# A retention layer and two feed-forward layers on one core: the decays of v and of the state as GpSimd multiplications

## The chip, the core and the metric

The kernel runs on one core of one Trainium2 chip. A core has a matrix engine (TensorE; PE in the profile, PEld for its weight loads), three engines for elementwise work (VectorE or DVE, ScalarE or ACT, GpSimd or POOL), a queue engine that issues most transfers (SyncE, SP), and 16 DMA engines that all queues share. The metric is device time in microseconds of one execution, as the median of several; lower is better.

## The reference

```python
scores = q @ k.T / sqrt(64)                      # q, k, v: 8 batches, 8 heads, 576 positions, 64 wide
gamma = 1 - 2.0 ** (-5 - head)                   # one decay per head
ret = scores * where(i >= j, gamma ** (i - j), 0)
x = (ret @ v) as 4608 tokens x 512
h = x @ w_in;  x = (h - tanh(h)) @ w_out         # first feed-forward layer, 512 -> 2048 -> 512
h = x @ w_in2; out = (h * sigmoid(1.702 * h)) @ w_out2   # second one
```

The decay is separable: `gamma ** (i - j)` is a factor of the key's position times a factor of the query's position. The kernel puts the key's factor on v.

## The kernel before, in words

**Chunks of the retention.** Each batch's 576 positions are cut into five chunks of 128, 128, 128, 128 and 64, so there are 40 chunks, and the first four of them (all of batch 0) are done ahead of the feed-forward work. For a chunk the kernel loads kT, qT, v and k (`att_load`), multiplies v by its decay (`att_decay`), multiplies kT by qT into `pj` and masks it into `pm` on VectorE (`att_scores`), and then (`att_values`) adds two products into `op`: `pm` with the decayed v, and, from the second chunk of a batch on, the state `S` with qT. A third product, `up`, of k with the decayed v is added to the old state (L352), and the sum is multiplied by gamma to the 128th (L353): this is the state for the next chunk. `op` times `dq` is the chunk's output, `xf` for the tokens of the first tile and `xe` later. A chunk whose decayed v is late holds up its `up` and its `op`; a late state holds up the `op` of the next chunk.

**Who multiplies v.** For the first eight chunks it is one VectorE instruction (L295; 512 elements a partition, 256 for a batch's last chunk). From the ninth on it is ScalarE, one instruction for each head or pair of heads (L300: eight of 64 elements, four for a last chunk). The state is decayed on VectorE always.

**Layer 1.** A tile is 512 tokens. Its x is cut into a 16-bit high half `xh` (ScalarE, L186) and low half `xl` (VectorE, L187), the weights likewise into `wih`, `wil`, `woh`, `wol`, and each product is taken as three matmuls (high-high, low-high, high-low): L464 for `h`, L626 for `y`. The weights come as 64-bit numbers, in 16 pieces of 1 MB (eight of w_in, eight of w_out, called units): `unit_join` puts one together into a 32-bit `w` (ScalarE L176 and, for w_out, L180; VectorE L178, L181, L182), `unit_split1` cuts it into halves (L186, L187). A unit's load waits for a buffer that an earlier join has to free. All this runs in the first tile, beside chunks 4 to about 8. `act1` makes the activation: two tanh and a square on ScalarE (L477, L478, L481), a product (L482) and the halves `gh` and `gl`. The `h` banks are two: the third block of 12 `h` matmuls waits until ScalarE has read both tanh of the first block, and so on.

**Layer 2** begins at about 800 us (L520, L555) and takes no part in the change.

**What sets the order.** The program is written as a list of steps, but a scheduler that plans with its own timings orders the instructions of each engine, and each engine then works strictly in that order. To hold the scheduler back, the code writes one element of a tile that a later instruction fills, from a value that must be there first: such a pin makes the later instruction wait. Two loads have pins on GpSimd (L158: one element of `xf` copied into `f`). Where TensorE would be idle in the first 31 us, matmuls on a tile of zeros (`idle`, L704 and L719) keep it busy.

Of the kernel before, what the change touches and what calls it, by code (L numbers as in the profile page):

```python
# [17 lines left out]
AF = mybir.ActivationFunctionType  # L18
ALU = mybir.AluOpType
# [5 lines left out]
B, H, S, D = 8, 8, 576, 64  # L25
NT, DM, DFF = 4608, 512, 2048
P = 128
# [4 lines left out]
NPAIR = H // 2  # L32
CHUNKS = [(s0, min(P, S - s0)) for s0 in range(0, S, P)]
# [22 lines left out]
LEAD = 4  # L56
# [39 lines left out]
def small_h(ctx: ExitStack, tc: tile.TileContext, w1i, w1o, w2i, w2o, qt, kt, k, v, dq_d,  # L96
            dv_d, mask_d, dg_d, out, flag):
    nc = tc.nc
    V, A, G, PE, SP = nc.vector, nc.scalar, nc.gpsimd, nc.tensor, nc.sync
# [85 lines left out]
    def two(hi, lo, src, scale):  # L185
        A.activation(out=hi, in_=src, func=AF.Copy, scale=scale)  # L186
        V.scalar_tensor_tensor(out=lo, in0=src, scalar=scale, in1=hi, op0=ALU.mult, op1=ALU.subtract)  # L187

    def unit_split1(kind, p):
        o, w = L[1], L[1].raw.pop((kind, p))  # L190
        if kind == "i":
            b, u = divmod(p, 2)
            if not u:
                o.wih[b], o.wil[b] = (wp1.tile([P, KD, 512], F16, tag=f"{nm}{b}", name=f"{nm}1_{b}") for nm in ("wih", "wil"))
            hi, lo = (x[b][:, :, u * 256 : u * 256 + 256] for x in (o.wih, o.wil))
        else:
            b, u = divmod(p, 4)
            if not u:
                o.woh[b], o.wol[b] = (wp1.tile([P, 8, DM], F16, tag=f"{nm}{b}", name=f"{nm}1_{b}") for nm in ("woh", "wol"))
            hi, lo = (x[b][:, 2 * u : 2 * u + 2, :] for x in (o.woh, o.wol))  # L200
        two(hi, lo, w, SW)

    def unit_most1(kind, p):
# [62 lines left out]
    def ps_tile(pp, stage, name):  # L266
        p, tag = pp[stage]
        return p.tile([P, NPAIR, P], F32, tag=tag, name=name)

    def ps_two(pp, stage, name):  # L270
        p, tag = pp[stage]
        return p.tile([P, 2, NPAIR, P], F32, tag=tag, name=name)
# [17 lines left out]
    def att_decay(b, n):  # L290
        s0, T = CHUNKS[n]
        a = att[b, n]
        if b * len(CHUNKS) + n < 2 * LEAD:
            x, w = (0, H) if T == P else (H, NPAIR)
            V.tensor_tensor(out=a.v[:, :w], in0=a.v[:, :w], op=ALU.mult,  # L295
                            in1=dg[:, x : x + w].rearrange("p (a b) -> p a b", b=1).to_broadcast([P, w, D]))
            return
        for h in range(H if T == P else NPAIR):
            x = h if T == P else H + h
            A.activation(out=a.v[:, h], in_=a.v[:, h], func=AF.Copy, scale=dg[:, x : x + 1])  # L300

    def att_scores(b, n, pp, pin=None):
        s0, T = CHUNKS[n]
# [20 lines left out]
    def att_values(b, n, pp):  # L324
        s0, T = CHUNKS[n]
        a = att.pop((b, n))
        op = ps_two(pp, "v", "op")
        state = att.get((b, "S"))

        def add(w, x, c0, c1, start, stop):  # L330
            for hp in range(NPAIR):
                q, c = divmod(hp, 2)
                for j in range(2):
                    PE.matmul(op[64 * c : 64 * c + 64, j, q, c0:c1], w(hp, j), x(hp, j), start=start and not q, stop=stop and q == 1)  # L334

        half = lambda j: slice(64 * j, 64 * j + 64)
        if n:
            add(lambda hp, j: state[half(j), hp, :], lambda hp, j: a.qT[half(j), hp, :T], 0, T, True, False)
        if T == P:
            add(lambda hp, j: a.v[half(j), NPAIR * j + hp, :], lambda hp, j: a.p[j][half(j), hp, :64], 0, 64, not n, False)  # L340
            add(lambda hp, j: a.v[:, NPAIR * j + hp, :], lambda hp, j: a.p[j][:, hp, 64:], 64, P, False, True)
        else:
            add(lambda hp, j: a.v[half(j), hp, :], lambda hp, j: a.p[0][half(j), hp, :T], 0, T, not n, True)
        if n + 1 < len(CHUNKS):
            up = ps_tile(pp, "u", "up") if pp is not late else op[:, 0, 2:].rearrange("p a (b d) -> p (a b) d", b=2)
            for hp in range(NPAIR):
                for j in range(2):
                    PE.matmul(up[half(j), hp, :D], a.k[:, NPAIR * j + hp, :], a.v[:, NPAIR * j + hp, :], start=True, stop=True)  # L348
        if n + 1 < len(CHUNKS):
            new = ap.tile([P, NPAIR, D], F32, tag="S", name="S")  # L350
            if n:
                V.tensor_tensor(out=new, in0=up[:, :, :D], in1=state, op=ALU.add)  # L352
            V.tensor_tensor(out=new, in0=new if n else up[:, :, :D], op=ALU.mult,  # L353
                            in1=dg[:, H + NPAIR :].rearrange("p (a b) -> p a b", b=1).to_broadcast([P, NPAIR, D]))
            att[b, "S"] = new
        by_bank = lambda x, at: x.rearrange("p (j q) t -> p j q t", j=2)[:, :, :, at : at + T]
        done, g0 = 0, b * S + s0
        if g0 + T <= TT:

            if not x_first:  # L360
                x_first.append(yp.tile([P, KD, TT], F32, tag="yf", name="xf"))
            V.tensor_tensor(out=by_bank(x_first[0], g0), in0=op[:, :, :2, :T], in1=by_bank(dq, 0), op=ALU.mult)
            return
        e = ap.tile([P, NPAIR, P], F32, tag="xe", name="xe", bufs=1)
        if n + 1 < len(CHUNKS):
            V.tensor_copy(out=e[:, 0, :1], in_=new[:, 0, :1])
        V.tensor_tensor(out=by_bank(e, 0), in0=op[:, :, :2, :T], in1=by_bank(dq, 0), op=ALU.mult)
        while done < T:
            ti, off = divmod(g0 + done, TT)
            m = min(T - done, TT - off)  # L370
            SP.dma_start(x_d[ti][:, :, off : off + m], e[:, :, done : done + m])
            done += m
# [293 lines left out]
    dg = ac.tile([P, H + 2 * NPAIR], F32, name="dg")  # L666
# [11 lines left out]
    early = {"s": (ps_y, "y"), "v": (ps_a, "a"), "u": (ps_h, "h")}  # L678
# [3 lines left out]
    units1 = deque([("i", 0), ("i", 1), ("o", 0)])  # L682
# [8 lines left out]
    def next_join(after=None):  # L691
        unit_join(1, *units1[0], wb, after)
        next_load()

    def next_split():
        unit_split1(*units1.popleft())

    warm = cp.tile([P, TT], F16, name="warm")
    V.memset(warm, 0.0)
# [21 lines left out]
    for i in range(-2, LEAD):  # L721
        if i + 2 < LEAD:
            att_decay(*chunks[i + 2])
        if 0 <= i + 1 < LEAD:
            att_scores(*chunks[i + 1], early)
        if i >= 0:
            att_values(*chunks[i], early)
            if i == 0:
                att_load(*beyond[NIP])
                for x in range(2):  # L730
                    next_load(tp, x_first[0][:1, x, :1])
            if i in (1, LEAD - 1):
                fill(att[0, "S"][:1, 0, :1], 5 if i == 1 else 12)
        if i == 2:
            after = [att[0, LEAD - 1].p[-1][:1, 0, :1]]
# [2 lines left out]
        pre.popleft()()  # L738
    for i in range(2):
        next_join(after[i])  # L740
        next_split()
    for i in range(1, LEAD):
        att_load(*beyond[i + NIP])
    bg = deque()
    for i, ch in enumerate(chunks[LEAD:]):
        def begin(ch=ch, nxt=beyond[LEAD + i + NIP - 1] if i else None):
            if nxt:
                att_load(*nxt)
            att_decay(*ch)

        bg.append(begin)
        pp = middle if i < 2 else late
        pin = (lambda: att[0, "S"][:1, 0, :1], lambda: newest[0][:1])[i] if i < 2 else None
        bg.append(lambda ch=ch, pp=pp, pin=pin: att_scores(*ch, pp, pin))
        bg.append(lambda ch=ch, pp=pp: att_values(*ch, pp))
# [6 lines left out]
    for i in range(n1 + LAG):  # L762
        if i < n1:
            t, p = steps[i]
# [3 lines left out]
            for _ in range(2 if len(pre) > KF // 2 - p else 1):  # L768
                if pre:
                    pre.popleft()()  # L770
            work = [f for _ in range(2 if units1 else 0) for f in (next_join, next_split)]
            if bg:
                n = min(6 if t == 0 else 5, len(bg))
# [46 lines left out]
        if i >= LAG:  # L820
            t, p = steps[i - LAG]
# [4 lines left out]
    for n in range(LAG, NTILE * KF // 2):  # L826
        t, p = divmod(n, KF // 2)
# [827 lines left out]
```

## Time and profile before

| | |
|---|---|
| median of 3 runs | 1558.76 us (1558.08 to 1559.37) |
| the profiled execution | 1558.13 us, of which its span is 1556.4 us |
| PE busy | 1531.8 us (98%) |
| DVE, ACT busy | 1082.1 us (70%), 823.1 us (53%) |
| POOL busy | 4.9 us in 18 instructions |

Rows of a timeline begin with the start and the duration in us, then the engine, the line of the kernel, the operation and the tiles (out<-in), and in brackets how long the engine had been idle before and what ended that. Durations of instructions that follow each other overlap a little, so the distance from start to start is what one costs.

### The profile page before, as it was taken

Reading aid. Unit: us, or ns where it says so; the run is one execution under the profiler, and the core shown is the slowest. Engines: PE = TensorE matmul, PEld = TensorE weight load, DVE = VectorE, ACT = ScalarE, POOL = GpSimd, SP = SyncE. Lnnn points to the kernel's source line nnn. Section 1 sums busy time; section 2 is a strip of 40 time slices with the busy share of each in tenths; the row PEclk is TensorE's granted clock in tenths of the full one; section 3 lists DMA queues with packets and bytes.
Section 4 is the critical chain, followed back from the end, with each engine's and each line's share of the span. In section 5 each row is a group of like instructions: output and inputs, shape, how many; then the busy total and the mean of one; then the engine's idle time right before and its main releaser. Section 6 shows DMA issues by size and latency. Waiting matters only on the chain.

```text
span 1556.4 us, 29515 instructions
## 1 busy us (share of the span) xinstructions
PE 1531.8 (98%) x12347; PEld 1024.0 (66%) x12347; DVE 1082.1 (70%) x1720; ACT 823.1 (53%) x1441; POOL 4.9 (0%) x18
## 2 busy tenths in 40 slices
PE   7999999999999999999999999999999999999998
PEld 4444555555554544444444588888888888888887
DVE  6984535554443438888776499797888888887865
ACT  3995545455455446778676455354544454454432
POOL 0000000000000000000000000000000000000000
PEclk9999999999999999999999999999999999999999
DMA  9663324233323124444428243433434433432310
GB/s 356 219 197 123 118 74 155 73 105 109 112 79 106 51 92 138 170 162 156 158 101 310 85 150 116 152 123 123 150 119 127 141 127 119 140 129 99 133 62 30
DMA packets 107983, 205.84 MB, mean 132 GB/s; under 512 B 24640, under 2 KB 47808, under 8 KB 105664
## 3 DMA queue, kind: packets, MB, share of 16 engines
q1 hardware_dynamic: 107552, 203.72, 39.4%
q8 instruction: 99, 1.62, 0.4%
q14 instruction: 44, 0.36, 0.1%
q10 hardware_dynamic: 288, 0.14, 0.0%
HBM read 161.88 MB, written 41.94 MB: 131 GB/s over the span
## 4 chain that ended last, share of the span: by engine, by line
PE 91%; ACT 3%; DVE 1%; DMA 1%; issue 0%; ACTq 0%; SPq 0%; DVEq 0%
PE y L626 22%; PE h L464 22%; PE pr L520 21%; PE yp L555 20%; PE op L334 2%; PE pj L316 2%; PE yk L555 1%; PE op L348 1%; DMA f<-in_moe_w_out 1%; ACT w L176 1%; ACT v L300 0%; ACT u L481 0%; ACT u L477 0%; ACT wih L186 0%; ACT w L180 0%
## 5 line engine op out<-in xcount | busy, mean ns | idle before, releaser
L520 PEld LDWEIGHTS <-ws 128*128 128x128 f16 x3024 | 295.9, 98 | 36.5 <-issue 1.7
L464 PE MATMUL h<-xh,wih 128*128 128x512 f16 x576 | 218.2, 379 | 2.2 <-ACT wih L186 1.9
L464 PE MATMUL h<-xl,wih 128*128 128x512 f16 x576 | 218.2, 379 | 0.8 <-DVE xl L187 0.8
L626 PE MATMUL y<-gl,woh 128*128 128x512 f16 x576 | 218.5, 379 | 0.0
L626 PE MATMUL y<-gh,wol 128*128 128x512 f16 x576 | 218.4, 379 | 0.0
L464 PE MATMUL h<-xh,wil 128*128 128x512 f16 x576 | 217.9, 379 | 0.4 <-DVE wil L187 0.4
L626 PE MATMUL y<-gh,woh 128*128 128x512 f16 x576 | 218.2, 379 | 0.0
L520 PE MATMUL pr<-th,ws 128*128 128x256 f16 x1152 | 217.4, 273 | 0.3 <-DVE u L534 0.2
L626 PEld LDWEIGHTS <-woh 128*128 128x128 f16 x1152 | 112.2, 98 | 133.0
L464 PEld LDWEIGHTS <-wih 128*128 128x128 f16 x1152 | 111.0, 98 | 133.3 <-ACT wih L186 2.0
L482 DVE TENSOR_TENSOR wt<-u,wt 128x1024 f32<-128x1024 f32 x72 | 88.1, 1224 | 150.6 <-ACT u L481 150.6
L555 PE MATMUL yp<-wo,gh 128*128 128x256 f16 x1152 | 186.8, 273 | 0.0
L520 PE MATMUL pr<-bh,ws 128*128 128x256 f16 x864 | 170.4, 273 | 0.0
L477 ACT ACTIVATE u<-h 128x512 f32<-128x512 f32 x144 | 84.9, 590 | 158.2 <-PE h L464 158.1
L536 ACT ACTIVATE gs<-u,isig 128x1024 f32<-128x1024 f32 x72 | 82.5, 1146 | 142.6 <-DVE u L535 142.6
L520 PE MATMUL pr<-tl,ws 128*128 128x256 f16 x576 | 157.0, 273 | 0.0
L555 PE MATMUL yp<-wo,gl 128*128 128x256 f16 x576 | 135.4, 273 | 0.0
L186 ACT ACTIVATE gh<-gs,sg 128x1024 f16<-128x1024 f32 x72 | 82.7, 1149 | 91.5 <-DVE gs L539 91.3
L555 PE MATMUL yp<-wo,ringwoh 128*128 128x256 f16 x768 | 126.2, 273 | 0.0
L555 PEld LDWEIGHTS <-gh 128*128 128x128 f16 x1152 | 112.7, 98 | 13.0
L520 PE MATMUL pr<-bl,ws 128*128 128x256 f16 x432 | 117.4, 273 | 0.0
L186 ACT ACTIVATE gh<-wt 128x1024 f16<-128x1024 f32 x72 | 76.0, 1055 | 73.7 <-DVE wt L482 73.5
(141 smaller groups left out, 2317.7 us busy)
## 6 DMA issues: line engine op xcount, KB each, us to landing
ws<-pd SPq DMA_DIRECT2D x144, 448.0 KB, 3.9
f<-in_moe_w_in SPq DMA_DIRECT2D x16, 1024.0 KB, 5.8
f<-in_moe_w_out SPq DMA_DIRECT2D x16, 1024.0 KB, 5.1
yd<-ev SPq DMA_DIRECT2D x36, 256.0 KB, 2.6
yf<-yd SPq DMA_DIRECT2D x9, 1024.0 KB, 5.7
out<-ev SPq DMA_DIRECT2D x36, 256.0 KB, 2.6
kT<-t_k SPq DMA_DIRECT2D x32, 256.0 KB, 2.9
qT<-t_q SPq DMA_DIRECT2D x32, 256.0 KB, 2.8
```

The costliest lines, as they stand in the source:

```text
L176: A.activation(out=half[:, :, 1].bitcast(F16), in_=part[:, :, 3].bitcast(BF16), func=AF.Copy)
L186: A.activation(out=hi, in_=src, func=AF.Copy, scale=scale)
L316: PE.matmul(o, a.kT[hs, hp, :T], a.qT[hs, hp, :T], start=True, stop=True)
L334: PE.matmul(op[64 * c : 64 * c + 64, j, q, c0:c1], w(hp, j), x(hp, j), start=start and not q, stop=stop and q == 1)
L348: PE.matmul(up[half(j), hp, :D], a.k[:, NPAIR * j + hp, :], a.v[:, NPAIR * j + hp, :], start=True, stop=True)
L464: PE.matmul(h, w, x[:, kd, :], start=n == 0, stop=n == 3 * KD - 1)
L477: A.activation(out=u[:, x], in_=h, func=AF.Tanh, scale=isig * NARROW)
L482: V.tensor_tensor(out=w, in0=u, in1=th, op=ALU.mult)
L520: PE.matmul(ps, w, x[:, xi, k, :], start=i == 0, stop=i == 5)
L536: A.activation(out=gs.rearrange("p (a b) n -> p a b n", b=2)[:, 0:4:3], in_=h.rearrange("p (a b) n -> p a b n", b=2), func=AF.Gelu_apprx_s ...
L555: PE.matmul(bank[:, m], ops[a][:, x, m * P : m * P + P], L[2].out[w][:, p, wi, :], start=start and m == 0 and r == 0, stop=stop and m == 1 ...
L626: PE.matmul(ys[m], a, b, start=first and i == 0, stop=last and i == 2)
```

## The change

v's decay is one multiplication for every chunk, on GpSimd for all but the very first chunk of all (`b or n`), which stays on VectorE. ScalarE no longer has a part in it. The state's decay goes to GpSimd for the second to fourth chunk of batch 0 (`n and pp is early`). The first unit's low halves get a pin: one element of `wil` is written from `after[1]`, the last element of `xf`, so that VectorE makes `wil` only behind chunk 3's output. Nothing else changes in the program as written, but the scheduler orders the first tile anew.

```diff
-    def unit_split1(kind, p):
+    def unit_split1(kind, p, after=None):
...
+        if after is not None:
+            V.tensor_copy(out=lo[:1, 0, :1], in_=after)
         two(hi, lo, w, SW)
...
     def att_decay(b, n):
         s0, T = CHUNKS[n]
         a = att[b, n]
-        if b * len(CHUNKS) + n < 2 * LEAD:
-            x, w = (0, H) if T == P else (H, NPAIR)
-            V.tensor_tensor(out=a.v[:, :w], in0=a.v[:, :w], op=ALU.mult,
-                            in1=dg[:, x : x + w].rearrange("p (a b) -> p a b", b=1).to_broadcast([P, w, D]))
-            return
-        for h in range(H if T == P else NPAIR):
-            x = h if T == P else H + h
-            A.activation(out=a.v[:, h], in_=a.v[:, h], func=AF.Copy, scale=dg[:, x : x + 1])
+        x, w = (0, H) if T == P else (H, NPAIR)
+        (G if b or n else V).tensor_tensor(out=a.v[:, :w], in0=a.v[:, :w], op=ALU.mult,
+                                           in1=dg[:, x : x + w].rearrange("p (a b) -> p a b", b=1).to_broadcast([P, w, D]))
...
-            V.tensor_tensor(out=new, in0=new if n else up[:, :, :D], op=ALU.mult,
-                            in1=dg[:, H + NPAIR :].rearrange("p (a b) -> p a b", b=1).to_broadcast([P, NPAIR, D]))
+            by = G if n and pp is early else V
+            by.tensor_tensor(out=new, in0=new if n else up[:, :, :D], op=ALU.mult,
+                             in1=dg[:, H + NPAIR :].rearrange("p (a b) -> p a b", b=1).to_broadcast([P, NPAIR, D]))
...
-        next_split()
+        next_split(None if i else after[1])
```

GpSimd's order at the start of the program, before (`mask` is the mask of the short chunks, the two L158 are the pins of two weight loads, `ISA` at L137 loads the code of the all-reduce that follows):

```order
L709 COPY mask_133<-mask 64x64 x2
L158 COPY f_289<-xf 1x1
L158 COPY f_292<-xf 1x1
L137 ISA
L137 ISA arx<-m_7677 128x1
```

and now (`v_1` to `v_4` are the v of chunks 1 to 4, `v_0_492` that of chunk 5; the ISA at L296 loads the code that the multiplications need, and that of the all-reduce is loaded behind the last of them):

```order
L707 COPY mask_133<-mask 64x64 x2
L296 ISA
L296 TENSOR_TENSOR v_1_198<-v_1_198,dg 128x512
L296 TENSOR_TENSOR v_2_206<-v_2_206,dg 128x512
L158 COPY f_289<-xf 1x1
L158 COPY f_292<-xf 1x1
L351 TENSOR_TENSOR S<-S,dg 128x256
L296 TENSOR_TENSOR v_3_214<-v_3_214,dg 128x512
L296 TENSOR_TENSOR v_4_287<-v_4_287,dg 128x256
L351 TENSOR_TENSOR S<-S,dg 128x256 x2
L296 TENSOR_TENSOR v_0_492<-v_0_492,dg 128x512
```

The pins of the two loads now stand behind two multiplications, and the decay of chunk 2's state (the first of the two S rows) stands behind v of chunk 4, as it did on VectorE.

VectorE's order from chunk 2's output to chunk 3's, before:

```order
L362 TENSOR_TENSOR xf<-op,dq 128x4x128
L352 TENSOR_TENSOR S<-up,S 128x256
L171 COPY w_465<-pm 1x1
L295 TENSOR_TENSOR v_4_287<-v_4_287,dg 128x256
L353 TENSOR_TENSOR S<-S,dg 128x256
L178 TENSOR_SCALAR w_465<-f_218 128x1024
L352 TENSOR_TENSOR S<-up,S 128x256
L181 TENSOR_SCALAR f_218<-f_218 128x1024
L353 TENSOR_TENSOR S<-S,dg 128x256
L182 SCALAR_TENSOR_TENSOR w_465<-f_218,w_465 128x1024
L311 COPY pj_564<-S 1x1
L362 TENSOR_TENSOR xf<-op,dq 128x4x128
```

and now, two rows further (`w_465` is the first unit, `w_478` the second):

```order
L360 TENSOR_TENSOR xf<-op,dq 128x4x128
L349 TENSOR_TENSOR S<-up,S 128x256
L171 COPY w_465<-pm 1x1
L178 TENSOR_SCALAR w_465<-f_218 128x1024
L349 TENSOR_TENSOR S<-up,S 128x256
L181 TENSOR_SCALAR f_218<-f_218 128x1024
L182 SCALAR_TENSOR_TENSOR w_465<-f_218,w_465 128x1024
L308 COPY pj_565<-S 1x1
L360 TENSOR_TENSOR xf<-op,dq 128x4x128
L202 CAST wil_0_474<-xf 1x1
L171 COPY w_478<-xf 1x1
L187 SCALAR_TENSOR_TENSOR wil_0_474<-w_465,wih_0_473 128x4x256
```

Three multiplications have left this stretch, and the second L349 waits for GpSimd now, with all that stands behind it.

ScalarE's order behind the halves of x, before (`w_552` is the first unit of w_out, `w_477` the second of w_in, `w_576` the third):

```order
L176 ACTIVATE w_552<-f_289 128x1024
L180 ACTIVATE w_552<-f_289 128x1024
L176 ACTIVATE w_477<-f_220 128x1024
L186 ACTIVATE woh_0_560<-w_552 128x1024
L477 ACTIVATE u<-h 128x512
L478 ACTIVATE wt<-h 128x512
L481 ACTIVATE u,energy<-u 128x512
L186 ACTIVATE wih_0_473<-w_477 128x4x256
L477 ACTIVATE u<-h 128x512
L478 ACTIVATE wt<-h 128x512
```

and now (the same units are `w_553`, `w_478` and `w_577`):

```order
L176 ACTIVATE w_478<-f_220 128x1024
L176 ACTIVATE w_553<-f_289 128x1024
L180 ACTIVATE w_553<-f_289 128x1024
L186 ACTIVATE wih_0_473<-w_478 128x4x256
L186 ACTIVATE woh_0_561<-w_553 128x1024
L475 ACTIVATE u<-h 128x512
L476 ACTIVATE wt<-h 128x512
L176 ACTIVATE w_577<-f_292 128x1024
L479 ACTIVATE u,energy<-u 128x512
L475 ACTIVATE u<-h 128x512
L476 ACTIVATE wt<-h 128x512
```

The second unit's high halves come ahead of the first block's activation, which both used to precede them, and a join's L176 has come between the first block's tanh and the second's.

## Rows read from the trace of the kernel before

**Rows 1.** Busy us by stage: PE, PEld, DVE, ACT, POOL, clock, DMA, GB/s

```profile
20.00:31.00 11.00, 6.87 (x92) 4.57 (x89) 8.22 (x16) 4.94 (x6) 0.00 (x0) 0.84 1.07 376
39.00:60.00 21.00, 20.18 (x135) 10.28 (x136) 20.38 (x29) 21.00 (x39) 0.00 (x0) 1.00 0.57 172
100.00:118.50 18.50, 14.80 (x79) 6.89 (x78) 15.15 (x20) 16.28 (x29) 0.00 (x0) 1.00 0.45 149
```

**Rows 2.** Waits of PE after 31 us: total us, times, longest

```profile
PE op L334 <- DVE pm L321: 3.0, 2, 2.2
PE pj L316 <- issue: 1.5, 1, 1.5
```

**Rows 3.** The chain of work, 0 to 120 us: start, us, what

```profile
41.75 1.25 ACT w L176
43.01 1.20 ACT w L180
47.14 0.49 ACT wt L478
48.47 2.03 ACT v L300 x8
...
59.32 0.63 DVE f L181
...
61.67 1.15 DVE w L182
...
81.74 2.00 ACT v L300 x8
...
96.54 5.25 DMA f<-in_moe_w_out
...
106.31 1.91 ACT v L300 x8
```

**Rows 4.** Timeline of POOL, the first 13 us

```profile
4.66 0.51 POOL L709 COPY mask<-mask 64x64 f32<-64x64 f32 x2 [4.23 <-DMA mask<-c_mask]
12.23 0.29 POOL L158 COPY f<-xf 1x1 int32<-1x1 int32 x2 [7.07 <-DVE xf L362]
```

**Rows 5.** Instructions of L137: durations in ns, first and last start

```profile
L137 POOLq MODIFY_POOL_CONFIG  x2: 1/1/1, 12.5 to 12.6; - x2
```

**Rows 6.** Transfers issued in the first 14 us: KB, us to landing

```profile
v<-n_v SPq DMA_DIRECT2D x4, 256.0 KB, 5.6
...
kT<-t_k SPq DMA_DIRECT2D x1, 128.0 KB, 10.3
```

**Rows 7.** Timeline of all engines, 9 to 32 us

```profile
9.69 0.69 DVE L295 TENSOR_TENSOR v<-v,dg 128x512 f32<-128x512 f32 x1 [1.99 <-DMA v<-n_v]
...
18.25 0.67 PE L334 MATMUL op<-qT,S 64*64 64x128 f32 x16 [1.10 <-DVE xf L362]
...
23.73 0.43 DVE L295 TENSOR_TENSOR v<-v,dg 128x256 f32<-128x256 f32 x1 [2.25 <-DMA v<-n_v]
...
24.07 0.42 DVE L353 TENSOR_TENSOR S<-S,dg 128x256 f32<-128x256 f32 x1
...
24.63 1.13 PE L334 MATMUL op<-qT,S 64*64 64x128 f32 x16 [4.13 <-DVE S L353]
...
25.51 1.78 PE L334 MATMUL op<-pm,v 64*64 64x64 f32 x32
...
27.23 3.07 PE L719 MATMUL idle<-warm 128*128 128x512 f16 x12
...
27.50 0.67 DVE L362 TENSOR_TENSOR xf<-op,dq 128x512 f32<-128x512 f32 x1
...
28.57 1.99 ACT L186 ACTIVATE xh<-xf 128x1024 f16<-128x1024 f32 x2
...
29.90 1.20 DVE L187 SCALAR_TENSOR_TENSOR xl<-xf,xh 128x1024 f16<-128x1024 f32 x1
```

**Rows 8.** Timeline of PE: the third block of h

```profile
39.03 0.39 PE L464 MATMUL h<-xh,wih 128*128 128x512 f16 x1 [1.86 <-ACT wih L186]
```

More of the change, by code (lines that the diff above doesn't have):

```diff
@@ L693, in next_join, with next_split @@
         next_load()
-    def next_split():
-        unit_split1(*units1.popleft())
+    def next_split(after=None):
+        unit_split1(*units1.popleft(), after)
     warm = cp.tile([P, TT], F16, name="warm")
```

## The prediction

> **What bounds the kernel now.** I read the page first: PE is busy for 98% of the span, so no more than the 25 us in which it idles can be won, and the change touches only the first 560 us. Then I read where the idle time lies. In the first 31 us PE follows the loads; from 31 us on it waits only for VectorE and ScalarE, and only in the first tile: 1.86 us before the third block of h, which waits for ScalarE [rows 8], and, between 90 and 118.5 us, 3.0 us in two waits for VectorE's mask and 1.5 us before one pj [rows 2]. Behind 119 us no wait of layer 1 is left, so whatever ScalarE or VectorE gains there is worth nothing. Third I read the two engines by stage: from 39 to 60 us ScalarE is busy for 21.0 of 21.0 us and VectorE for 20.38; from 100 to 118.5 us PE has only 14.80 of 18.5, ScalarE 16.28 and VectorE 15.15 [rows 1]. They bound the first tile together, joining and cutting weights. Last the chain of waits: ScalarE's v decays lie on it three times, 2.03, 2.00 and 1.91 us [rows 3].
>
> **The change, part by part.** The sum is made against the profiled execution, 1558.13 us; the median is 0.63 above it.
>
> *The price of a GpSimd multiplication.* No such row exists. GpSimd's copies of 64 elements take 0.51 us for two, its copies of one element 0.29 for two [rows 4]: 0.255 and 0.145 each, so 1.7 ns an element, and 1.0 us for 512 and 0.6 for 256, the values that I take. Below stands VectorE's own 0.69 us [rows 7], above ScalarE's 2.03 us for the same work [rows 3].
>
> *The code load.* GpSimd now loads code between its mask copies, which end at 5.17 us [rows 4], and v of chunk 1, which lands at 9.69 [rows 7]. Before, the load's records of 1 ns stand at 12.5 us [rows 5] and nothing followed for 800 us, so its cost is not seen. It lies between nothing and 10.3 us, the longest transfer of that stretch; the nearest row is the median transfer, 5.6 us [rows 6], and I take that: ready at 10.8 us, v of chunk 1 done at 11.8 instead of 10.4. This lateness of 1.4 us is hidden: chunk 2's op waits 1.10 us for xf in any case, and chunk 3's op waits 4.13 us at 24.63 [rows 7], so only what exceeds some 5 us comes through. The two pins come at about 14 us instead of 12.2 [rows 4]; on SP their loads stand behind that of chunk 4's v, so they lose nothing. The Trainium skill ("GPSIMD Engine Reference", section 2.1) gives about 6 us for the first call after a load, which no run here shows yet; by it v of chunk 1 would be done at 12.2 us and the sum would stay.
>
> *The wait at 24.63 us.* It is VectorE's order: the state of chunk 2 stands behind v of chunk 4, which lands at 23.73, and op starts 0.90 later [rows 7]. The change doesn't take this away, since on GpSimd the state stands behind the same v. v 0.6, state 0.6, and the 0.14 that lay between the state's end and op (24.07 + 0.42 to 24.63): op starts 1.34 after the landing, 0.44 later than now, with bounds of 0 (VectorE's prices) and +1.2. Chunk 3's xf was 0.2 behind the end of its op (25.51 + 1.78 to 27.50) and gives that back, so xf is 0.3 late, and ScalarE, which still has the first high halves to make, starts xh at most 0.1 late. But VectorE makes xl now behind two pins, `wil` and the next join's L178, where xl came straight behind `wil` at 29.90 [rows 7], and TensorE's filling matmuls are shifted with op. I put the stream of h at +0.5.
>
> *The third block of h.* ScalarE is free at 30.56 + 0.1 (28.57 + 1.99) [rows 7]. The new order gives it L176 twice and L180, 1.25 + 1.25 + 1.20 [rows 3], until 34.35. VectorE's L181 (0.63) must follow that L180, then a mask of chunk 4 and L182 twice, 1.15 each [rows 3]: 37.6. ScalarE's `woh` (1.0, as one of the two xh) ends at 38.6 and the two tanh, 0.49 each, at 39.6. Only then is the bank of the third block free, which began at 39.03 [rows 8]. So the earlier `wih` wins nothing: the wait for it becomes a wait for the bank, and PE is 0.6 late there. A join's L176 now stands between the tanh of the first and of the second block, so I carry +0.7 to 60 us, start included, with bounds of -1.9 (the wait simply goes) and +2.5.
>
> *From 60 to 118.5 us.* ScalarE loses 2.00 + 1.91 us on the chain, and the 2.03 at 48.47 before it [rows 3]. The three PE waits, 4.5 us [rows 2], are for VectorE instructions that themselves wait for ScalarE's joins, so they shrink by what ScalarE gains. They can't all go: a weight load of 5.25 us, issued when a buffer comes free, stands on the chain too [rows 3], and ScalarE was idle there. I take two thirds, -3.0, between 0 and -4.5.
>
> *Behind that* 28 chunks go from ScalarE to GpSimd beside a PE that does not wait: 0. GpSimd's second code load, for the all-reduce, comes at about 560 us with 270 us to spare: 0. The state's decays of chunks 1 and 3 and VectorE's saved multiplications in the first 31 us: 0, since those instructions wait for loads.
>
> Sum: 1558.13 + 0.7 - 3.0 = 1555.8; with the median's 0.63, 1556.4 us.
>
> **The rivals.**
>
> *The order is better than I walked it.* If VectorE's join comes out early enough, the 1.86 us go too, with nothing lost at the start, and all 4.5 us behind: -6.1 with +0.3 for the state, 1552.7 us. For it speaks that VectorE loses seven v decays in its first 43 us and that the scheduler moved `wih` forward; against it that the bank needs ScalarE, which has no gap.
>
> *GpSimd's work holds up VectorE.* No row shows the two at work together for longer than a copy of one element. If each multiplication keeps VectorE waiting for its 1.0 us, then chunks 5 to 8 put 4.0 us on a VectorE that has 0.6 us of idle time between 39 and 60 us [rows 1], and chunks 9 to 11 take back two thirds of what ScalarE gives: +3.4 + 0.7 - 1.0, or 1561.9 us, slower. It decides from about 0.6 us per multiplication; below that VectorE's idle 3.35 us from 100 to 118.5 [rows 1] takes it. The Trainium skill ("SBUF — State Buffer", section "Who interferes with whom" and the reading of its diagram) has such a rule: the two share a port pair under an exclusive lock, which a VectorE instruction with two SBUF inputs wants too, and the loser waits for the whole instruction. By that rule xl, `wil`, L182 and the product L482 would be held, masks from PSUM not; no run here shows it.
>
> *The code load is long.* The transfers of that stretch already fill the DMA engines. From a load of some 9.5 us on, v of chunk 1 eats up the two waits, and every further us is late at the first h: at 13 us +3.5. TensorE's granted clock is a part of this: it was 0.84 on average from 20 to 31 us [rows 1], which is 3.5 us at the lower level, 1.2 GHz, behind the 4.13 us wait, and a longer wait means more of the fillers at that level. 1561.5 us.
>
> *The waits are where the loads put them*, and ScalarE's gain turns into waiting for weights: about 1558.8 us. I count this to the forecast's case, as its slow edge.
>
> **Chances.** The forecast with its slow edge 0.40, the better order 0.30, VectorE held 0.17, the long load 0.13. A measurement of this kernel tells some 0.2% from no change, 3.1 us. Faster by more than that: the better order and a little of the forecast, 0.33. Slower by more: about half of the two slow rivals and a remainder, 0.18. Within: 0.49. The range that should hold 8 in 10 is 1551.5 to 1562.5 us; the forecast's own is 1554 to 1559.5.
>
> **What would show it.** Right: GpSimd's 512-element rows at 0.7 to 1.3 us; v of chunk 1 done by 15 us; chunk 3's op at 25.0 to 25.4; the third block of h at 39.3 to 40 behind a tanh, not behind `wih`; less than 2 us of PE waits between 60 and 118.5 us. Wrong: VectorE's L182 or L187 longer than 1.2 us, or idle gaps before them, while GpSimd multiplies; a wait of PE on GpSimd before 18 us that reaches the first h; a granted clock below 1.00 behind 31 us; the third block of h at 37.5 us.

## The result: 1569.99 us, slower by 0.7%

The changed kernel takes 1569.99 us (median of 4, 1568.68 to 1570.94), the kernel before, on the same chip, 1559.07 (1558.08 to 1559.84): a ratio of 1.0069, 95% interval 1.0053 to 1.0085, or +10.8 us. The forecast was 1556.4 us, its range ended at 1562.5.

| profiled execution | before | changed |
|---|---|---|
| span, us | 1556.4 | 1567.2 |
| first h that needs `xl`, us | 31.62 | 37.79 |
| third block of h, us | 39.03 | 45.39 |
| first h of tile 1 that waits for `xl`, us | 133.91 | 144.20 |
| busy us of ScalarE, VectorE, GpSimd | 823, 1082, 5 | 771, 1084, 49 |

ScalarE lost 52 us of work and VectorE gained none worth telling; nevertheless 6.2 us are lost ahead of the first h, 4.1 more until tile 1, and 0.5 behind it. Tile 1's row, before and changed:

```profile
133.91 0.38 PE L464 MATMUL h<-xl,wih 128*128 128x512 f16 x1 [0.81 <-DVE xl L187]
```

```profile
144.20 0.38 PE L462 MATMUL h<-xl,wih 128*128 128x512 f16 x1 [0.65 <-DVE xl L187]
```

First the stages of the changed kernel, with the columns of [rows 1] (the mean granted clock stands behind the engines):

```profile
10.00:20.00 10.00, 2.85 (x42) 2.59 (x42) 1.95 (x4) 0.00 (x0) 2.90 (x6) 0.78 1.05 383
20.00:31.00 11.00, 8.75 (x190) 7.10 (x188) 5.95 (x11) 1.57 (x2) 3.17 (x5) 0.89 1.07 374
39.00:60.00 21.00, 18.09 (x127) 9.11 (x125) 20.00 (x25) 18.18 (x28) 2.09 (x2) 1.00 0.46 155
80.00:100.00 20.00, 17.61 (x139) 8.59 (x137) 16.16 (x19) 15.27 (x22) 1.58 (x1) 0.91 0.79 271
100.00:118.50 18.50, 17.14 (x134) 8.40 (x132) 17.27 (x19) 16.20 (x22) 1.56 (x1) 1.00 0.56 200
118.50:140.00 21.50, 19.96 (x163) 10.21 (x164) 11.06 (x17) 8.75 (x17) 1.52 (x1) 0.92 0.40 123
```

From 10 to 20 us PE has 2.85 us of work; the ten microseconds are gone before anything of the first tile runs. ScalarE is no longer full from 39 to 60 us (18.18 of 21.0, where [rows 1] had 21.00), and PE is still less busy (18.09 for 20.18): the relief did not reach it. And the clock falls below 1.00 twice behind 31 us.

Next the largest of PE's waits over the whole span (total us, times, longest); [rows 2] has before's behind 31 us, [rows 7] those at the start:

```profile
PE up L345 <- POOL v L296: 7.2, 1, 7.2
PE h L462 <- ACT wt L476: 4.3, 3, 2.1
PE pj L313 <- issue: 2.9, 1, 2.9
PE h L462 <- DVE xl L187: 2.3, 2, 1.7
PE op L331 <- POOL S L351: 2.2, 1, 2.2
```

The largest is new and is for GpSimd's first multiplication. The timeline shows where it comes from (the first row is the load's records; then start, us, engine, line, and in brackets the idle time before and its releaser; L331 is before's L334, L351 its L353, L345 its L348):

```profile
L296 POOLq MODIFY_POOL_CONFIG  x2: 7/7/7, 5.3 to 5.4; - x2
...
4.81 0.51 POOL L707 COPY mask<-mask 64x64 f32<-64x64 f32 x2 [4.38 <-DMA mask<-c_mask]
...
16.64 2.04 POOL L296 TENSOR_TENSOR v<-v,dg 128x512 f32<-128x512 f32 x2 [11.32 <-issue]
...
17.72 1.12 PE L345 MATMUL up<-v,k 128*64 128x64 f32 x16 [7.15 <-POOL v L296]
...
18.77 2.08 PE L313 MATMUL pj<-qT,kT 64*128 64x128 f32 x16
...
27.00 0.92 PE L345 MATMUL up<-v,k 128*64 128x64 f32 x24
...
28.42 0.42 DVE L349 TENSOR_TENSOR S<-up,S 128x256 f32<-128x256 f32 x1
...
28.91 1.19 POOL L351 TENSOR_TENSOR S<-S,dg 128x256 f32<-128x256 f32 x1 [4.84 <-DVE w L171]
...
30.16 0.67 PE L331 MATMUL op<-qT,S 64*64 64x128 f32 x16 [2.25 <-POOL S L351]
...
37.79 0.38 PE L462 MATMUL h<-xl,wih 128*128 128x512 f16 x1 [1.70 <-DVE xl L187]
...
45.39 0.38 PE L462 MATMUL h<-xh,wih 128*128 128x512 f16 x1 [1.71 <-ACT wt L476]
```

GpSimd is idle for 11.32 us between its mask copies and the first multiplication. The load's records stand at the head of that gap, at 5.3 us, and v of chunk 1 lands at 9.48, so for its last 7.2 us the multiplication waits for nothing but the load. Within PE's wait for it, at 15.6 us, the granted clock falls to 0.50, 1.2 GHz instead of 2.4, and stays there until 22.4 us, so 16 pj matmuls take 2.08 us instead of 1.16. Chunk 3's op starts at 30.16 instead of 24.63 [rows 7].

### The profile page after: what moved, and what is told of

It reads as the page before. It is cut to its first block, busy times and chain, and to the rows that moved or that the text cites. A ratio compares the mean times of both kernels' runs of the same rounds, so it can differ in the third digit from the quotient of the medians.

```text
span 1567.2 us, 29347 instructions
## 1 busy us (share of the span) xinstructions
PE 1536.9 (98%) x12347; PEld 1025.8 (65%) x12347; DVE 1083.8 (69%) x1711; ACT 771.0 (49%) x1213; POOL 49.2 (3%) x60
## 4 chain that ended last, share of the span: by engine, by line
PE 92%; DVE 3%; DMA 2%; ACT 1%; issue 1%; SPq 0%; POOL 0%; ACTq 0%; DVEq 0%
PE y L624 23%; PE h L462 22%; PE pr L518 21%; PE yp L553 20%; PE op L331 3%; PE pj L313 2%; PE yk L553 1%; PE op L345 1%; DMA f<-in_moe_w_in 1%; DMA v<-n_v 1%; DVE w L182 1%; DMA k<-n_k 0%; ACT w L176 0%; SPq L287 0%; DVE f L181 0%
```

## The experiments

My theory after the traces: the load makes the start late, by 6.2 us at the first h, and the rest is lost in the first tile. The rivals: the order of the work or GpSimd beside VectorE, with the load innocent; or the late start alone, with the tile's losses as its consequence. None of the kernels below leaves work out. Ratios are to the kernel before, with 95% intervals.

**E1, the load asked for early.**

```diff
+    code = cp.tile([P, 1], F32, name="code")
+    G.memset(code, 1.0)
+    G.tensor_tensor(out=code, in0=code, in1=code, op=ALU.mult)
     for t, src in ((dg, dg_d), (mask, mask_d)):
```

> The changed kernel, with one more GpSimd multiplication of one element per partition as its first work, which needs none of the inputs: whatever GpSimd has to load for a first multiplication is then asked for at about 0.5 us instead of 5.3. Theory (the 11.3 us ahead of the first multiplication is a load of code, and it alone sets the late start): the load ends by 12 us, chunk 1's v is multiplied by 13 us instead of 17.7, PE's wait of 7.15 us falls below 3, the first h stands at 31.5 to 33.5 us instead of 37.8, and the time is 1564 to 1566 us, since about 4.5 us of the loss lie in tile 0 and stay. Rival (the order of the start's work and GpSimd beside VectorE set it, not the load): the first h stays behind 36 us and the time at 1569 to 1571.

Measured: 1566.64 us, 1.0037 (1.0025 to 1.0049), 0.6 us above what theory gave; the six executions spread from 1562.66 to 1569.04, and the profiled one is the slowest of them. The load's records, GpSimd's timeline and PE's longest wait:

```profile
L705 POOLq MODIFY_POOL_CONFIG  x2: 11/11/11, 0.8 to 0.9; - x2
...
0.72 0.10 POOL L704 MEMSET code<- 128x1 f32 x1 [0.29 <-POOLq L1617]
8.92 0.18 POOL L705 TENSOR_TENSOR code<-code 128x1 f32<-128x1 f32 x1 [8.09 <-issue]
...
25.30 1.13 PE L331 MATMUL op<-qT,S 64*64 64x128 f32 x16 [5.92 <-POOL S L351]
```

The same gap stands in front of a multiplication of one element that needs no input, so it is the load, and not v or its queue. It is over at 8.92 us and the first h is back at 32.36. But half of the loss stays, with a first h only 0.7 us later than before's. So the first h does not set the time; the load is one cause of two. What PE waits for is now the state behind chunk 4's v (5.92 us at 25.30).

**E2, the start back on VectorE; E3, only ScalarE's part; E4, only the start's part.**

```diff
E2  -        (G if b or n else V).tensor_tensor(...
E2  +        (G if b * len(CHUNKS) + n >= LEAD else V).tensor_tensor(...
E2  -            by = G if n and pp is early else V
E2  +            by = V
E3  (kernel before) -        for h in range(H if T == P else NPAIR): ... A.activation(...)
E3                  +        G.tensor_tensor(out=a.v[:, :w], ..., op=ALU.mult, in1=dg...)
E4  +        if b * len(CHUNKS) + n >= 2 * LEAD:
E4  +            for h in range(...): A.activation(out=a.v[:, h], ..., scale=...); return
```

> The changed kernel with the v decay of chunks 0 to 3 and all the state decays back on VectorE, as before the change; chunks 4 and later stay on GpSimd, and so does the pin. Theory: GpSimd's load still happens but nobody waits for it, so the first h stands at 31 to 32.5 us and the time is 1563 to 1566 us. If the load still takes bandwidth from the loads of the start, the first h is 1 to 3 us later than the kernel before's 31.62 all the same. Rival (the loss is in the order of tile 0 alone, the start is made up for later): 1569 to 1571. Rival (tile 0's two stretches at half clock were only the late start's doing): 1558 to 1560.

> The kernel before with one part of the change alone: ScalarE's v decays (chunk 8 on) as GpSimd multiplications; start, states and pin as before. Theory: the start is that of the kernel before (first h at 31.6 us); this part is what reorders 60 to 125 us, and if the two stretches at half clock come from it the time is 1561 to 1564 us. Rival (these stretches come from the late start, the part itself takes 3 us of PE's waits out): 1555 to 1557.5. No part in it at all: 1558.5 to 1559.5.

> The changed kernel with chunk 8 on back on ScalarE as before the change; start, states, chunks 4 to 7 and the pin as changed. Theory (start +6.2 us, the rest from the part that is taken back here): first h at 37.8 us, 1565 to 1566.5 us. Rival (all of the loss hangs on the start, its lateness brings the two stretches at half clock too): 1569 to 1571. Rival (what is late at the start is made up for in tile 0): 1559 to 1562.

Measured: E2 1558.32 us, 0.9991 (0.9982 to 1.0), first h 29.94; E3 1560.28, 1.0006 (0.9997 to 1.0015), first h 32.72; E4 1564.72, 1.0035 (1.0022 to 1.0049), first h 37.64. E2 met the third reading: everything that is lost hangs on the start's decays, and the load costs nothing visible where nobody waits (its records stand at 12.8 us, and the first multiplication, at 24.59, had waited for its v). E3 fell between its readings, 0.8 us above "no part" and 0.7 below theory: moving ScalarE's v decays, for which I had booked -3.0 us, shows no gain, +0.9 us with an interval of -0.5 to +2.3. E4 came 0.3 us below theory's range. Its start is the changed kernel's, and 5.5 us are lost by it; with ScalarE's part on top they are 10.8, although that part alone is worth nothing. So something in the first tile depends on both.

**E5, the pin alone; E6, early load and the states on VectorE; E7, E2 made late; E8, only chunks 4 to 7 and the pin.**

```diff
E5  (kernel before) +        if after is not None:
E5                  +            V.tensor_copy(out=lo[:1, 0, :1], in_=after)
E5                  ...
E6  (E1)  -            by = G if n and pp is early else V
E6        +            by = V
E7  (E2)  +    lag = cp.tile([P, NPAIR, D], F32, name="lag")
E7        ...
E7        +            for _ in range(6 if i == LEAD - 1 else 0):
E7        +                V.tensor_tensor(out=lag, in0=att[0, "S"], in1=att[0, "S"], op=ALU.mult)
E8  (E2)  +        if b * len(CHUNKS) + n >= 2 * LEAD: ... A.activation(...)   # as E4
```

> The kernel before with the pin alone (the first piece's low halves behind chunk 3's output); every decay where it was. In the run with the start back on VectorE the first h came at 29.94 us, 1.7 earlier than in the kernel before, with the pin and chunk 4's v on GpSimd. Theory (chunk 4's v off VectorE gives that, the pin nothing): first h at 31.3 to 32 us, 1558.5 to 1560 us. Rival (the pin gives it): first h at 30 to 30.8 us, 1557 to 1558.5.

> The kernel with the early load, and the state decays of the first chunks back on VectorE, so that no state stands behind chunk 4's v on GpSimd (PE waited 5.92 us for it there). Theory (the loss of the start is the load and that queue): PE's wait for the state falls below 3 us, the first h stands at 30 to 31.5 us, and the time is that of the run with the start back on VectorE, 1557.5 to 1560 us. Rival (the multiplications of chunks 1 to 3 on GpSimd cost VectorE so much, or tile 0 is late whatever the start does): 1563 to 1567, as with the early load alone (1566.64).

> The kernel with the start back on VectorE (1558.32 us, first h 29.94), with six idle VectorE multiplications of 256 elements behind chunk 3's state, five of them ahead of the first piece's low halves: a start late by some 2 us with no GpSimd in it, which puts the first h where the early load had it (32.36). Theory A (tile 0 takes a late start badly at this phase, whatever makes it late): 1563 to 1567 us, as the early load. Theory B (lateness passes one for one, the early load's other 6 us come from GpSimd in the start): 1560 to 1561. Theory C (it is made up for in tile 0): 1558 to 1559.

> The kernel with the start back on VectorE, and chunk 8 on back on ScalarE: what is left of the change are the v decays of chunks 4 to 7 on GpSimd and the pin. Theory (ScalarE's decays were worth nothing in tile 0, moving them cost 1 us in the run that moved them alone): first h at 29.9 us and 1556.5 to 1558 us, below the 1558.32 with them on GpSimd. Rival (moving them gained what the start now keeps): 1559 to 1561.

Measured: E5 1558.93 us, 1.0 (0.9991 to 1.0009), first h 31.75: the pin has no part. E6 1557.51, 0.9992 (0.9983 to 1.0001), at the lower end of theory's range, first h 29.02, a us earlier than given. E7 1558.83, 0.9999 (0.999 to 1.0008): inconclusive, since the six multiplications fell mostly into idle time, the first h came at 30.46 and the order of the first tile changed with them. E8 1557.92, 0.9992 (0.9983 to 1.0001), in theory's range, first h 28.09 (29.9 given); not told apart from E2.

E6 against E1 is the surprise: 7.0 us (1.0037 to 0.9992) for three multiplications of 0.6 us moved from GpSimd to VectorE, with v of chunks 1 to 3 still on GpSimd. I compared the orders. E1's is row for row the changed kernel's on PE, VectorE, ScalarE and SP. E6's is E2's on PE, ScalarE and SP, and differs from E1's throughout the first tile. The scheduler plans the whole tile anew when the states change engine.

**E9 and E10, the load and the order apart.** With the order fixed in pairs, these two fill a square.

```diff
E9  (changed kernel) -            by = G if n and pp is early else V
E9                   +            by = V
E10 (E1)  -        (G if b or n else V).tensor_tensor(...
E10       +        (G if b or 0 < n < LEAD else V).tensor_tensor(...
```

> The changed kernel with the first chunks' state decays back on VectorE and nothing else: GpSimd's load comes late, as in the changed kernel. Its order on PE, VectorE, ScalarE and SP is row for row that of the run with the early load and the states on VectorE (1557.51 us), so against that run only the load is moved. Theory (the order that the scheduler makes for the first tile once the states are on GpSimd costs about 6 us there, the late load the rest): the load holds chunk 1 up to 16 or 17 us, the first h comes at 34 to 36 us instead of 29.02, and lateness passes about one for one: 1561 to 1563.5 us. Rival A (the late load costs its whole lateness and brings the tile's other losses as well): 1566 to 1570. Rival B (tile 0 takes the lateness up, the order is all): 1557.5 to 1559.5.

> The kernel with the early load (1566.64 us), with chunk 4's v on VectorE, so that GpSimd's states no longer stand behind it. SP's order is that of the changed kernel throughout, ScalarE's too, and VectorE's and PE's in the first tile but for that v and two swaps of neighbours. It is the changed kernel's order with an early start. Theory (the order costs about 6 us between 60 and 125 us however early the start is, by weight loads that go out late): first h at 30.5 to 32.5 us, the last w_out load of the tile 8 us or more behind the one before it, 1563 to 1566.5 us. Rival (it was the wait behind chunk 4's v, 5.92 us, and the late start; the order is as good as the other): 1557.5 to 1560.

Measured: E9 1564.02 us, 1.0035 (1.0023 to 1.0047); E10 1564.13, 1.0035 (1.0022 to 1.0049), first h 33.33.

| ratio to before | load asked for at 0.8 us | load behind the mask copies |
|---|---|---|
| states on VectorE | E6 0.9992 | E9 1.0035 |
| states on GpSimd (the changed kernel's order) | E1 1.0037, E10 1.0035 | changed 1.0069 |

Each column and each row differs by 0.0032 to 0.0045 or 5 to 7 us. By way of E9 that is -1.2 us for E6 itself, +6.7 for the late load, +5.3 for the states, 10.8 together (0.0001 is 0.16 us); by way of E1 the states cost 7.0 and the late load 5.0, so the two add up to within 1.7 us, which the intervals allow. Neighbours in the square don't overlap in their intervals. E9 came 0.5 us above what theory gave, its first h (36.52) 0.5 late, and well below its rival; E10's time fell inside (its first h 0.8 us late of what I gave).

The price of the states is not the tile's alone. From the profiled executions, us:

| kernel | first h | first `xl` matmul of tile 1 | between |
|---|---|---|---|
| before | 31.62 | 133.91 | 102.3 |
| E6, states on VectorE, early load | 29.02 | 132.70 | 103.7 |
| E9, states on VectorE, late load | 36.52 | 138.87 | 102.4 |
| E10, states on GpSimd, v of chunk 4 on VectorE, early load | 33.33 | 140.30 | 107.0 |
| changed, late load | 37.79 | 144.20 | 106.4 |

With the states on GpSimd the tile itself is 3 to 4 us longer (111.8 in E1's profiled execution, its slowest), and its start is later too: 4.3 us (E10) and 3.3 (E1, 32.36) against E6. The changed kernel's start is 1.3 later than E9's, but its load took 1.3 us longer in that execution (11.32 for 10.01).

E4 bears on the tile's part: it has the late load and the states on GpSimd, in the changed kernel's order up to the first pieces of the tile, but another order behind them, and costs 1.0035, as E9 does. So GpSimd's three multiplications don't cost this wherever they stand; that the layout of the tile behind them does is what is left, argued and not shown, since E4 has ScalarE's v decays back as well. The load's side, E9 and then E6, one order:

```profile
15.22 2.04 POOL L296 TENSOR_TENSOR v<-v,dg 128x512 f32<-128x512 f32 x2 [10.01 <-DMA v<-n_v]
...
16.30 1.12 PE L345 MATMUL up<-v,k 128*64 128x64 f32 x16 [5.41 <-POOL v L296]
...
28.40 0.67 PE L331 MATMUL op<-qT,S 64*64 64x128 f32 x16 [1.53 <-DVE S L351]
...
36.52 0.38 PE L462 MATMUL h<-xl,wih 128*128 128x512 f16 x1 [1.67 <-DVE xl L187]
```

```profile
9.71 0.18 POOL L705 TENSOR_TENSOR code<-code 128x1 f32<-128x1 f32 x1 [8.88 <-issue]
...
21.19 0.67 PE L331 MATMUL op<-qT,S 64*64 64x128 f32 x16 [1.53 <-DVE S L351]
...
29.02 0.39 PE L462 MATMUL h<-xl,wih 128*128 128x512 f16 x1
```

The state waits 1.53 us in both, so that wait covers nothing of the lateness: 7.2 us at chunk 3's op become 7.5 at the first h.

**E11, a candidate below both.** E6 with chunk 8 on back on ScalarE (the lines of E4).

> A candidate below both kernels: early load, states on VectorE, v of chunks 1 to 7 on GpSimd, chunk 8 on back on ScalarE. Its order on PE, ScalarE and SP is that of the run with chunks 4 to 7 and the pin alone (1557.92). Theory (VectorE is the bound of the start and gets 2.1 us of multiplications less): first h at 27.5 to 28.2 us instead of 28.09, 1556.5 to 1558 us. Rival (the start waits for loads there, nothing is won): 1557.5 to 1558.5.

Measured: 1558.56 us, 0.9999 (0.999 to 1.0008), first h 27.94. The first h is where theory had it, 0.15 us ahead of E8's, and nothing is won: the time lies at the rival's upper end, 0.06 us beyond it. That the start waits for loads fits one row, PE's wait for a load of qT, 1.4 us for 1.1 in E8; more is not shown.

**E12 and E13, a weight buffer held back.** In the changed order the last w_out load of the first tile goes out 8.4 us (changed kernel), 10.7 (E1) and 8.4 (E10) behind the one before it, in E6 and E9 2.5 us. E1's VectorE, with the load on SP's queue:

```profile
102.88 0.71 DVE L181 TENSOR_SCALAR f<-f 128x1024 int32<-128x1024 int32 x1
...
106.50 0.70 DVE L181 TENSOR_SCALAR f<-f 128x1024 int32<-128x1024 int32 x1 [2.92 <-ACT w L176]
107.11 2.35 DVE L182 SCALAR_TENSOR_TENSOR w<-f,w 128x1024 int32<-128x1024 int32 x2
...
108.40 0.37 SPq L159 DMA_DIRECT2D f<-in_moe_w_out  x1
```

L182 is the last reader of `f`. The first unit's could follow its L181 at once, but in this order it stands behind the next unit's L181, which waits for ScalarE's L176 and by it for a landing; so the buffer is not free and the next load not out. One element written ties the two:

```diff
+        if (l, kind, p) == (1, "o", NU - 2):
+            V.scalar_tensor_tensor(out=f[:1, :1, 1], in0=L[1].raw["w"][:1, :1], scalar=0,
+                                   in1=f[:1, :1, 1], op0=ALU.bitwise_and, op1=ALU.bitwise_or)
         V.tensor_scalar(out=f[:, :, 1], in0=f[:, :, 1], scalar1=13, ...)
...
+        L[l].raw["w"] = w
```

> The kernel with the early load (1566.64 us), with one more instruction on VectorE: one element of the unit of w_out before the last is written from the unit before it (its own value, the other masked to nothing), so that VectorE ends the earlier unit's join (L182) ahead of the later one's L181. SP's order is unchanged; VectorE's differs in one place of 8 rows, PE's and ScalarE's by swaps there. In the early load's trace both L182 stand behind an L181 that waits 2.92 us for a landing, and the last w_out load goes out at 108.40. Theory (the changed order holds the weight buffer back there, and PE's wait of 4.5 us at 118.7 comes from it): the last load goes out at 104.5 to 106 us, the wait shrinks below 2.5 us, and the time is 1562.5 to 1564.5 us. Rival (the load was not what PE waited for): 1566 to 1567.5.

> The changed kernel (1569.99 us) with that same one instruction. Here the later unit had landed 2.2 us before, and L181 waits only 0.71 us, so theory has less to win: the last w_out load goes out at 108 to 108.8 us instead of 109.79, and the time is 1568 to 1569.5 us. Rival (not the release but the number of instructions behind it): 1569.5 to 1571.

Measured: E12 (on E1) 1564.17 us, 1.0034 (1.0023 to 1.0046); E13 (on the changed kernel) 1569.86, 1.0066 (1.0052 to 1.008). The load went out at 103.29 and 108.42, as wanted, and the wait before pj is 2.5 us in E12's trace for 4.5 in E1's. But E1's is its slowest execution and E12's its second fastest. E12's time is in theory's range, its median 2.5 us below E1's; the ratios differ by only 0.0003 and the intervals overlap, so a gain is not shown. E13's rival holds: nothing.

**E14, the tanh ahead of the join.** In the changed kernel PE's longest wait for a tanh and the first late fall of the clock stand together:

```profile
90.86 1.37 ACT L176 ACTIVATE w<-f 128x1024 f16<-128x1024 bf16 x1 [1.12 <-DMA f<-in_moe_w_in]
92.09 1.03 ACT L186 ACTIVATE woh<-w 128x1024 f16<-128x1024 f32 x1
...
93.51 0.59 ACT L476 ACTIVATE wt<-h 128x512 f32<-128x512 f32 x1
...
94.14 0.59 PE L462 MATMUL h<-xh,wih 128*128 128x512 f16 x1 [2.14 <-ACT wt L476]
...
94.95 0.63 PE L462 MATMUL h<-xh,wil 128*128 128x512 f16 x1
```

ScalarE waits for a weight load and only then makes the tanh that frees PE's bank; behind it the matmuls of 512 columns take 0.63 us for 0.38. In E9's order the tanh stands ahead of the same join, and no wait of PE lies between 60 and 97 us:

```profile
88.94 0.59 ACT L476 ACTIVATE wt<-h 128x512 f32<-128x512 f32 x1
...
90.35 1.38 ACT L176 ACTIVATE w<-f 128x1024 f16<-128x1024 bf16 x1 [0.21 <-DMA f<-in_moe_w_in]
```

```diff
+    L[1].raw["tanh"] = th[:, 1, :1]                 # in act1
...
+        if (l, kind, p) == (1, "i", 6):             # in unit_join
+            after = L[1].raw["tanh"][:1]
         if after is not None:
             V.tensor_copy(out=w[:1, :1], in_=after.bitcast(I32))
```

> The changed kernel (1569.99 us) with one pin more: the join of the seventh unit of w_in (its load goes out at 85.35 and lands at 90.86) is held behind the tanh of the pair before it. In the changed kernel's trace ScalarE takes the join first, and PE waits 2.14 us at 94.14 for a bank that this tanh frees, and the granted clock stands at half for 3.4 us behind it; in the run with the states on VectorE alone (1564.02) both tanh stand ahead of the join and neither is seen. Up to 86 us the order is the changed kernel's on every engine; behind it the scheduler orders the rest of the first tile anew. Theory (ScalarE's order there costs the wait and the clock, 3.8 us): no wait for that tanh, no half clock before 105 us, and 1565 to 1568 us. Rival (the time comes back as a later join, since the weights are the bound): the last w_out load later than 110 us, 1569 to 1571.

Measured: 1568.81 us, 1.0061 (1.0048 to 1.0075), between the two readings. PE's waits behind 60 us in E14:

```profile
90.74 0.38 PE L464 MATMUL h<-xh,wih 128*128 128x512 f16 x1 [1.48 <-ACT wt L478]
...
102.87 0.67 PE L333 MATMUL op<-qT,S 64*64 64x128 f32 x16 [2.57 <-DVE pm L320]
...
118.34 2.08 PE L315 MATMUL pj<-qT,kT 64*128 64x128 f32 x16 [2.76 <-issue]
```

The clock stays up at 95 us and the wait shrinks to 1.48 us, but one for VectorE's mask has come at 102.87, and the median is 1.2 us lower, inside the intervals. In the profiled execution the load took 9.84 us for 11.32 and the first h came at 35.53, 2.3 us early, ahead of anything that the edit touches; from there to tile 1 (141.98) it is 106.4 us, as in the changed kernel. So nothing is won in the tile. That is the rival's outcome; its sign, a last w_out load later than 110 us, was not met (109.48).

## Why the prediction was wrong, step by step

*The code load* is the step that failed first: taken at 5.6 us with 10.3 as the upper bound, the gap measured 11.32, and 9.84 to 10.96 in the four other kernels with the late load (E4, E9, E13, E14). I had read it off the transfers of [rows 6], and no row ties it to them. Asked for at 0.8 us, with no input to wait for, it took 8.0 to 8.9 us (8.09 in E1, 8.88 in E6, 8.39 in E10, 8.30 in E11, 7.96 in E12). The Trainium skill ("GPSIMD Engine Reference", section 2.1) gives about 6 us, without the wait for an event that lies inside; the early load measured 1.3 to 1.5 times that, and the late one, counted from v's landing, 5.6 (E14) to 7.2 us (changed).

*Its cover* failed too, and this is the larger part. I let 5 us be hidden by the waits of 1.10 and 4.13 us. PE's up of chunk 1 came 7.2 us late (17.72 for 10.49) and chunk 3's op 5.5 us (30.16 for 24.63): 1.7 were hidden. The 4.13 us could not go below the state's own chain, which stood inside them: `up` ends at 27.92, the sum starts at 28.42, the product ends at 30.10. The other wait was eaten by the clock, at half from 15.6 to 22.4 us. By my own rule (a late us for each one above 9.5) the load of 11.3 us would have cost 1.8, and E9's of 10.0 only 0.5; E9 is 6.7 us behind E6 and 5.5 behind the kernel before. The up of chunk 1 in the kernel before:

```profile
10.49 0.69 PE L348 MATMUL up<-v,k 128*64 128x64 f32 x16
```

*The state behind v* (+0.44 us) was right in kind where the load was early: E1's op starts at 25.30, 0.67 later than before. In the changed kernel v of chunk 4 is long done, and the state itself takes 1.19 us beside VectorE.

*The price* of a multiplication was right: 1.04 us for 512 elements, 0.61 for 256, alone. That is partly luck, since it was drawn out from copies of 64 elements with one input. Beside VectorE it is more: 1.2 to 2.0 us for 512 in the changed kernel.

*The third block of h* was right: the wait for `wih` became one for the tanh (1.71 us), and the start's lateness passed through.

*60 to 118.5 us, -3.0*, is the second step that failed. E3 puts this part at +0.9 us. The waits did not shrink with ScalarE's work. In E3 they are 2.5 us for a mask and 2.8 before a pj, where before had 3.0 and 1.5. In the changed kernel they moved: 2.14 us for a tanh, 2.90 before a pj (which starts 0.10 us behind VectorE's `xe`, so that is most likely what it waited for), each with the clock at half for 3.4 us behind it. I had walked the new order from 28 to 45 us by hand and then booked waits of the old order as reduced. That the order differed up to 125 us because three small multiplications changed engine, which made the start later and the tile 3 to 4 us longer, 5 to 7 us in all, I had in no rival. Nor was it so that no wait of layer 1 stood behind 119 us: before has one of 0.81 us at 133.91, for `xl`; the sum had nothing on it.

*The rivals.* The long load (0.13) was the right one in kind, and too small: 1561.5, a figure without a working, since +3.5 us on the forecast's 1556.4 gives 1559.9. Two signs of being wrong came as listed: PE's wait for GpSimd that ended at 17.72 us and reached the first h, and a clock below 1.00 behind 31 us. The port rule (0.17) exists but is not the sum. The changed kernel has a clear meeting:

```profile
116.14 0.70 DVE L181 TENSOR_SCALAR f<-f 128x1024 int32<-128x1024 int32 x1 [0.41 <-ACT w L176]
116.18 1.56 POOL L296 TENSOR_TENSOR v<-v,dg 128x512 f32<-128x512 f32 x1 [22.33 <-DMA v<-n_v]
116.75 1.26 DVE L351 TENSOR_TENSOR S<-S,dg 128x256 f32<-128x256 f32 x1
```

GpSimd's 1.04 became 1.56 us beside L181, and the state's 0.42 became 1.26, ending 0.27 behind GpSimd. The Trainium skill ("SBUF — State Buffer", "Who interferes with whom") says that the loser waits for the whole instruction; the rows agree to 0.15 us (GpSimd ends 0.90 behind L181, the state 0.27 behind GpSimd). A meeting costs VectorE 0.3 to 0.85 us, but E2 and E6 have them too (L178 takes 1.42 and 1.46 us there for 0.75), and their time is not above before's.

*What stays open* is which instruction of the changed order makes the tile 3 to 4 us longer. Two single hold-ups were taken away, and neither gave a gain beyond the intervals. The issue of the last w_out load runs with the time of the profiled execution in most runs: 96.8 to 100.4 us in E2, E6, E7, E8 and E11 (1556.7 to 1558.5 us), 103.3 to 106.5 in E4, E9, E10 and E12 (1562.2 to 1565.6), 108.4 to 109.8 in E1, E13, E14 and the changed kernel (1567.2 to 1569.9). The kernel before (102.82, 1558.1), E3 (103.73, 1560.6) and E5 (106.71, 1560.1) do not fit, so this is a mark and not a proof; a late start alone moves both.

No version beats the kernel before: E2, E6 and E8 stand at 0.9991 and 0.9992, with intervals that reach 1.0. All three are 0.8% below the changed kernel.

## What to carry to other kernels

The first multiplication on an engine that so far only copied may bring a load (8 to 11 us here); put a dummy of one element at the very start, or give the engine its first work where nobody waits. A wait is cover only down to the chain that runs inside it, so walk that chain before booking it. And where a scheduler orders the program, a small instruction that changes engine can be a new order for everything behind it: compare the orders, and separate the order's price from the instruction's by pairs of kernels that differ in one and share the other.

## What was not expected of the hardware

- The load differs with when it is asked for: 8.0 to 8.9 us from 0.8 us on, 9.8 to 11.3 behind the mask copies, up to 1.5 us apart in kernels with the same order there.
- In the changed kernel the granted clock fell to half for 3.4 us behind waits of PE of 2.14 and 2.90 us, and within the 7.15 us for 6.8 us, while behind the 2.25 us at 30.16 it stayed at 1.00. Behind the same wait in E14 (2.24 us, to 27.90) it fell to half from 29.5 to 32.9 us. So here the length of a wait does not tell what the clock does.
- GpSimd's multiplication of 512 elements took up to 3.0 us in E2: the first of two that took 4.50 us from 33.85 us on, beside VectorE's L182 (33.62) and L187 (34.75), against 2.04 for two alone.

```profile
33.85 4.50 POOL L296 TENSOR_TENSOR v<-v,dg 128x512 f32<-128x512 f32 x2 [7.67 <-DMA v<-n_v]
```
